# High and low parts of q and k made once per head pair in staging tiles and placed by DMAs

## The chip, the core and the metric

The kernel runs on one core of one Trainium2 chip. The metric is the device time of one execution in microseconds (us). The kernel before takes 946.16 us (median of 3 runs, 944.52 to 946.6). The engines that matter here are TensorE (PE in the profile, its weight loads PEld), VectorE (DVE), ScalarE (ACT), GpSimd (POOL) and SyncE (SP), which issues most of the DMAs. Each engine works through its own instructions in a fixed order and waits at the head of its queue for semaphores.

## The reference

Causal attention with a bias from a running sum, over 8 batches and 8 heads, 576 positions, 64 values a head; then a mixture of experts with one expert a token. Cut to what matters:

```python
scores = matmul(q, k.T) / sqrt(D)
cum = cumsum(maximum(s, 0)); bias = -(cum[..., :, None] - cum[..., None, :])
scores = where(causal, -1e9, scores + minimum(bias, 0))
attn = exp(scores - max(scores)); attn /= sum(attn) + 1e-9
x = matmul(attn, v)                       # (8*576, 512) after the heads are joined
e = argmax(x @ w_gate + modality_bias[modality_id]); gate = softmax prob of e
out[token] = gate * (relu(x @ w1[e]) @ w2[e])
```

## The kernel before, in words

The first part is attention. It goes over 32 head pairs: one head of two batches at a time (`ab` is 0 or 1). For a pair there are nine score tiles, taken in the order `ORDER`: four tiles of 128 queries for each of the two batches, with 128 to 512 keys, and tile 8 ("pep"), which holds the last 64 queries of both. A score is formed in float32r, which keeps only the high part of a float32, so q and k are split: a high part and the rest, the low part. Each tile takes two matmuls into one PSUM bank `sp`: `KA` times `QH` (128 rows: high k over low k, against high q twice) and `KB` times `QL` (76 rows: high k and the rows of the bias against low q and the rows that pick the bias). There are two sets of these four operands, `QH`, `QL`, `KA` and `KB`, used by turns.

After the two matmuls DVE takes the mask and the row minimum (L219, L233), ACT the exponential (L238), PE transposes the tile into a bank `pt` (L248, L257), ACT copies it to `PT` (L251; tile 8: DVE, L263). When all nine tiles of a pair are in `PT`, `tail` multiplies with V (L274 and L279, banks `ox` and `om`), ACT and DVE copy the result to `oT` (L283, L284, L287), PE transposes and projects it (L293, L296: in two groups, which use the one bank `ox` after each other) and DVE scales each group into `x` (L299, L301). `run` writes this with the scores three tiles ahead of the transposes and with the tail of a pair spread over the scores of the next; the order in which each engine finally gets its instructions is set by a scheduler that moves them by its own times, not by the text of `run` alone.

The operands are made in `prep`. [...] POOL makes the high parts of q and k (L174: two calls of 128x576 for `QH`, two for `KA`, two of 64x576 for `KB`) and the low parts (L192 for `KA`, L194 for half of `QL`); DVE makes the other half of `QL` (L188). The rows of the bias come by two small DMAs (L170, L171). `prep(pi + 1)` is written into the scores of pair `pi`. SP's queue carries, per pair, two loads of q and k of 576 KB each, V of 320 KB and the two small ones.

After every eighth pair `done` routes the tokens of two batches: DVE works out the expert of each token, POOL issues nine indirect DMAs (L502) that write the rows to lists in DRAM. The second part, the mixture of experts, works on blocks of 256 tokens of one expert and loads its weights by SP.

Of the kernel before, what the change touches and what calls it, by code (L numbers as in the profile page):

```python
# [7 lines left out]
F32 = mybir.dt.float32  # L8
F32R = mybir.dt.float32r
# [3 lines left out]
ALU = mybir.AluOpType  # L13
# [4 lines left out]
P = 128  # L18
KW = 576
# [11 lines left out]
class Attn:  # L31
# [3 lines left out]
    def __init__(self, ctx, tc, qkv, s, ident, consts):  # L35
        nc = tc.nc
        self.nc, self.tc, self.qkv, self.ident = nc, tc, qkv, ident
        c = self.const = ctx.enter_context(tc.tile_pool(name="aconst", bufs=1))
        self.dr = ctx.enter_context(tc.tile_pool(name="adr", bufs=1, space=DRAM))
        self.ld = ctx.enter_context(tc.tile_pool(name="ld", bufs=2))  # L40
        self.wk = ctx.enter_context(tc.tile_pool(name="wk", bufs=2))
        self.sm = ctx.enter_context(tc.tile_pool(name="sm", bufs=3))
        self.ps1 = ctx.enter_context(tc.tile_pool(name="ps1", bufs=2, space=PSUM))
        self.ps2 = ctx.enter_context(tc.tile_pool(name="ps2", bufs=1, space=PSUM))
        self.QH = [c.tile([P, 2, 640], F32R, name=f"QH{u}") for u in range(2)]
        self.QL = [c.tile([P, 2, 640], F32R, name=f"QL{u}") for u in range(2)]
        self.KA = [c.tile([P, 2, KW], F32R, name=f"KA{u}") for u in range(2)]
        self.KB = [c.tile([P, 2, KW], F32R, name=f"KB{u}") for u in range(2)]
        self.PT = [c.tile([P, PTW], F32, name=f"PT{u}") for u in range(3)]
        self.oT = [c.tile([P, 640], F32, name=f"oT{u}") for u in range(2)]  # L50
        self.pw = c.tile([P, 8, 2 * XW], F32, name="pw")
        self.mk = c.tile([P, 800], F32, name="mk")
        self.hold = [None]
        with tc.tile_pool(name="cst", bufs=1, side="right") as t1:
            sr = t1.tile([64, KW], F32, name="sr")
            nc.sync.dma_start(sr, s)
            raw = self.load_qk(0)
# [11 lines left out]
            self.raw = {0: raw}  # L69
            for _ in self.prep(0):  # L70
                pass

    def exts(self, t1, cum):

# [73 lines left out]
    def load_qk(self, pi):  # L148
        nc = self.nc
        raw = [self.ld.tile([P, 2, KW], F32, name="rawq"), self.ld.tile([P, 2, KW], F32, name="rawk")]  # L150
        for u in range(2):
            nc.sync.dma_start(raw[u], self.qkv[pi, :, 2 * KW * u:2 * KW * u + 2 * KW].rearrange("p (a k) -> p a k", a=2))
        return raw

    def load_v(self, pi):
        V = self.ld.tile([P, 2, 5, 64], F32, name="V", bufs=3)
        self.nc.sync.dma_start(V, self.qkv[pi, :, 4 * KW:].rearrange("p (a j d) -> p a j d", a=2, j=5))
        return V

    def load(self, pi):  # L160
        self.raw[pi] = self.load_qk(pi)
        self.V[pi] = self.load_v(pi)

    def prep(self, pi):
        nc = self.nc
        rq, rk = self.raw.pop(pi)
        QH, QL, KA, KB = (t[pi % 2] for t in (self.QH, self.QL, self.KA, self.KB))
        QHf, KAf = QH.bitcast(F32), KA.bitcast(F32)
        if pi:
            nc.sync.dma_start(KB.bitcast(F32)[64:74], self.ekd.rearrange("(a p) r k -> p r a k", a=2)[pi])  # L170
            nc.sync.dma_start(QL.bitcast(F32)[74:76, :, :KW], self.eqd.rearrange("(a p) r k -> p r a k", a=2)[pi])  # L171

        def high(o, i, e=None):
            (e or nc.gpsimd).tensor_scalar(o, i, 1.0, 1.0, ALU.mult, ALU.mult)  # L174

        lo, up = slice(0, 64), slice(64, P)
        for a in range(2):
            if pi:
                high(QH[:, a, :KW], rq[:, a])
            else:  # L180
                nc.scalar.copy(QH[:, a, :KW], rq[:, a])
        yield
        for a in range(2):
            high(KA[:, a], rk[:, a], nc.vector if pi == 0 and a == 0 else None)
        yield
        for a in range(2):
            if a == 0:
                nc.vector.tensor_tensor(QL[lo, a, :KW], rq[lo, a], QHf[lo, a, :KW], ALU.subtract)  # L188
            high(KB[lo, a], rk[lo, a], nc.vector if pi == 0 and a == 0 else None)
            yield  # L190
        for a in range(2):
            i = (nc.vector if pi == 0 and a == 0 else nc.gpsimd).tensor_tensor(KA[up, a], rk[up, a], KAf[up, a], ALU.subtract)  # L192
            yield
        (nc.vector if pi == 0 else nc.gpsimd).tensor_tensor(QL[lo, 1, :KW], rq[lo, 1], QHf[lo, 1, :KW], ALU.subtract)  # L194
        yield
# [108 lines left out]
    def run(self, npair, newx, done, setup):  # L304

        bg = []
        self.load(1)
        seq = [(pi, i) for pi in range(npair) for i in ORDER]
        sts = {}
        prev, prepg, n = None, None, len(seq)  # L310
        for k in range(n + LAG + 9):
            if k < n:
                pi, i = seq[k]
                if k % 9 == 0:
                    sts[pi] = self.start(pi, newx(pi // 8) if pi % 8 == 0 else sts[pi - 1]["x"])
                    prepg = self.prep(pi + 1) if pi + 1 < npair else None
                self.score(sts[pi], i)
                if k in setup:
                    with ExitStack() as after:
                        for h in self.hold:  # L320
                            after.enter_context(self.tc.issue_after(h))
                        setup[k]()
                if k % 9 == 7 and pi + 2 < npair:
                    self.load(pi + 2)
                if prepg is not None:
                    next(prepg, 0)
            nt = None
            if LAG <= k < n + LAG:
                p0, i0 = seq[k - LAG]
                if i0 == ORDER[-1]:  # L330
                    nt = sts[p0]
            if prev is not None:
                if next(prev, 0) == 0:
                    prev = None
                    if ps["pi"] % 8 == 7:
                        bg.append(done(ps["pi"] // 8, ps["x"]))
            if LAG <= k < n + LAG:
                self.trans(sts[p0], i0)
            if nt is not None:
                prev, ps = self.tail(nt), nt  # L340
            if prev is None and k >= n + LAG:
                break
            if bg and next(bg[0], 0) == 0:
                bg.pop(0)
        assert prev is None
        return bg


def pack(q, k, v, s):

    out = np.zeros((32, 128, 4 * KW + 640), np.float32)
    for bp in range(4):
        for h in range(8):
            o = out[bp * 8 + h]
            for ab in range(2):
                b = 2 * bp + ab
                qT, kT = q[b, h].T, k[b, h].T

                qq = qT if ab == 0 else np.concatenate([qT[:, 512:], qT[:, :512]], 1)
                for r in (0, 64):  # L360
                    o[r:r + 64, KW * ab:KW * ab + KW] = qq
                    o[r:r + 64, KW * (2 + ab):KW * (3 + ab)] = kT
                vv = np.zeros((640, 64), np.float32)
                vv[:576] = v[b, h]
                v0 = 4 * KW + 320 * ab
# [611 lines left out]
```

## Time and profile before

| | us |
|---|---|
| median of 3 runs | 946.16 |
| the profiled execution's own time | 941.79 |
| its span, first to last instruction | 940.1 |
| first reduction of scores (L219) in the span | 29.71 |
| last scaling into x (L301) of the last pair ends | 465.31 |
| PE busy, 42 to 142 us | 99.24 of 100 |
| PE busy, 465 to 900 us | 422.86 of 435 |

The views give times in us from the span's start. In a row of the timeline stand the start, the duration, the engine, the line, the operation and the tiles; in brackets how long the engine was idle before and what ended that. A row of the windows gives each engine's busy time in a stretch, with the number of instructions, then the clock that TensorE was granted, the share of the DMA engines' time and what they moved. SPq is SP's queue of DMA issues.

### The profile page before, as it was taken

How to read it: one execution, taken by the hardware profiler on the slowest of the kernel's cores; microseconds unless marked ns; L12 is line 12 of the kernel's file. 1: busy time of each engine (PE TensorE's matmuls, PEld its weight loads, DVE VectorE, ACT ScalarE, POOL GpSimd, SP SyncE). 2: the span in 40 equal slices, each digit the busy share in tenths (PEclk: the TensorE clock that was granted, in tenths of full speed). 3: DMA queues.
4: the chain of work that ended last, by engine and by line, in shares of the span. 5: the costliest groups of instructions: out<-in, count | busy, mean ns of one | idle time of the engine just before them, and what ended most of it. 6: DMA issues, size and time to landing. Idle time of an engine off the chain costs nothing. (4 is left out here: it accounts for less than half of the span.)

```text
span 940.1 us, 16721 instructions
## 1 busy us (share of the span) xinstructions
PE 860.9 (92%) x5584; PEld 714.7 (76%) x5584; DVE 633.8 (67%) x1485; ACT 527.5 (56%) x1209; POOL 576.1 (61%) x478
## 2 busy tenths in 40 slices
PE   0799999799989998899988989999999999999984
PEld 0577777577667777677777979999999999999862
DVE  7477777577856778777556966566665566566771
ACT  3577776577656775587644525445544454454551
POOL 9576667666786766885064725556655465564760
PEclk9999999899999999999999999999999999999998
DMA  5743334533363335550577757666666666665940
GB/s 149 205 121 135 134 135 133 181 132 113 121 213 118 104 120 171 187 179 18 189 244 263 280 190 290 238 231 223 247 227 220 225 225 228 225 230 224 325 157 3
DMA packets 67564, 172.79 MB, mean 184 GB/s; under 512 B 12087, under 2 KB 12087, under 8 KB 67412
## 3 DMA queue, kind: packets, MB, share of 16 engines
q1 hardware_dynamic: 61620, 151.64, 47.1%
q0 software_dynamic: 5856, 20.06, 5.4%
q8 instruction: 45, 0.74, 0.3%
q14 instruction: 43, 0.35, 0.1%
HBM read 144.95 MB, written 26.80 MB: 183 GB/s over the span
## 5 line engine op out<-in xcount | busy, mean ns | idle before, releaser
L238 ACT ACTIVATE pe<-pe,mx 128x512 f32<-128x512 f32 (+3 forms) x256 | 143.8, 563 | 54.1 <-DVE mx L219 50.7
L279 PE MATMUL om<-PT,V 128*64 128x448 f32 (+3 forms) x640 | 124.9, 424 | 10.7 <-DVE PT L263 10.5
L791 ACT ACTIVATE hT<-hp 128x512 fp32r<-128x512 f32 x72 | 42.8, 595 | 156.9 <-PE hp L789 156.9
L251 ACT COPY PT<-pt 128x512 f32<-128x512 f32 (+3 forms) x256 | 106.7, 421 | 36.1 <-PE pt L248 28.9
L248 PE MATMUL pt<-ident,pe 128*128 128x128 f32 x640 | 121.9, 288 | 4.0 <-DVE PT L263 3.3
L219 DVE CUSTOM_DVE_ANT_0 pe<-sp,mk 128x512 f32<-128x512 f32 (+3 forms) x256 | 114.7, 478 | 12.9 <-PE sp L217 7.3
L775 POOL DMA_INDIRECT out<-ys,oi x36 | 37.3, 1037 | 133.5 <-DVE ys L774 50.5
L216 PE MATMUL sp<-KA,QH 128*128 128x256 f32 (+2 forms) x256 | 97.0, 386 | 20.1 <-DVE KA L192 16.0
L248 PEld LDWEIGHTS pt<-ident,pe 128*128 128x128 f32 x640 | 79.2, 146 | 40.5 <-issue 14.9
L174 POOL TENSOR_SCALAR QH<-rawq 128x576 fp32r<-128x576 f32 x62 | 47.0, 761 | 88.7 <-issue 80.9
L192 POOL TENSOR_TENSOR KA<-rawk,KA 64x576 fp32r<-64x576 f32 x63 | 95.9, 1541 | 2.6
L217 PE MATMUL sp<-KB,QL 76*128 76x256 f32 (+2 forms) x256 | 86.4, 343 | 7.3 <-DMA QL<-oh 7.3
L789 PE MATMUL hp<-xT,wcb 128*128 128x256 f32 x648 | 90.2, 283 | 1.6 <-DVE hT L792 1.6
L279 PEld LDWEIGHTS om<-PT,V 128*64 128x64 f32 x640 | 60.7, 136 | 40.6 <-DVE PT L263 14.9
L789 PEld LDWEIGHTS hp<-xT,wcb 128*128 128x128 f32 x648 | 83.6, 189 | 2.5 <-DVE hT L792 1.9
L792 DVE SCALAR_TENSOR_TENSOR hT<-hp,hT 128x512 fp32r<-128x512 f32 x72 | 49.2, 684 | 52.9 <-ACT hT L791 52.9
L789 PE MATMUL hp<-xT,wcc 128*128 128x256 f32 x528 | 76.4, 285 | 8.3 <-DVE hT L792 3.2
L768 PE MATMUL y<-wcb,hT 128*128 128x512 f32 x336 | 81.1, 398 | 0.0
L789 PE MATMUL hp<-xT,wca 128*128 128x256 f32 x552 | 78.1, 284 | 0.4 <-ACT xT L754 0.3
L789 PEld LDWEIGHTS hp<-xT,wcc 128*128 128x128 f32 x528 | 69.9, 194 | 9.3 <-DVE hT L792 3.4
L768 PEld LDWEIGHTS y<-wcb,hT 128*128 128x128 f32 x336 | 62.8, 188 | 14.8
L789 PEld LDWEIGHTS hp<-xT,wca 128*128 128x128 f32 x552 | 71.7, 190 | 1.3 <-ACT xT L754 0.5
(270 smaller groups left out, 1987.7 us busy)
## 6 DMA issues: line engine op xcount, KB each, us to landing
wrbw<-in_w SPq DMA_DIRECT2D x104, 512.0 KB
wraw<-in_w SPq DMA_DIRECT2D x56, 512.0 KB
rawq<-in_qkv SPq DMA_DIRECT2D x32, 576.0 KB
rawk<-in_qkv SPq DMA_DIRECT2D x32, 576.0 KB
xg<-lists SPq DMA_DIRECT2D x18, 576.0 KB
V<-in_qkv SPq DMA_DIRECT2D x32, 320.0 KB
lists<-z SPq DMA_DIRECT2D x8, 576.0 KB
ekd<-ek SPq DMA_DIRECT2D x1, 1440.0 KB
```

The lines of the kernel that those rows point to most:

```text
L174: (e or nc.gpsimd).tensor_scalar(o, i, 1.0, 1.0, ALU.mult, ALU.mult)
L192: i = (nc.vector if pi == 0 and a == 0 else nc.gpsimd).tensor_tensor(KA[up, a], rk[up, a], KAf[up, a], ALU.subtract)
L216: nc.tensor.matmul(sp[:, :nn], QH[:, q0:q0 + P], KA[:, ab, :nn], start=True, stop=False)
L217: nc.tensor.matmul(sp[:, :nn], QL[:EXT, q0:q0 + P], KB[:EXT, ab, :nn], start=False, stop=True)
L219: ins = nc.vector.tensor_tensor_reduce(out=t[:, :n], in0=sp[:, :n], in1=self.mk[:, 512 - n:512], scale=-0.125, scalar=3.0e38, op0=ALU.add, ...
L238: nc.scalar.activation(t[:, :n], t[:, :n], AF.Exp, bias=m, scale=-1.0, accum_out=st["sums"][:, i:i + 1])
L248: nc.tensor.transpose(out=pt[:, P * j:P * j + P], in_=pe[:, P * j:P * j + P], identity=self.ident)
L251: cp(w[:, :, v:v + P], pt[:, :P * (c + 1)].rearrange("p (j q) -> p j q", q=P))
L279: nc.tensor.matmul(om[r, q0 - P:], V[:, ab, j, :], PT[ab][:, PTS * j + q0 if j < 4 else PTW - 64:PTS * j + KW if j < 4 else PTW], start=j ...
L768: self.last[0] = nc.tensor.matmul(y[u], hT[:, a, f, P * u:P * u + P], W[4 + f // 2][:, c, 512 * (f % 2):512 * (f % 2) + 512], start=f == 0 ...
L789: nc.tensor.matmul(hp[:, u], W[k][:, a, f:f + P], xT[:, c, k], start=k == 0 and i == 0, stop=k == 3 and i == 2)
L792: nc.vector.scalar_tensor_tensor(hT[:, 1, 2 * m:2 * m + 2], hp, 0.0, hs.bitcast(F32), ALU.max, ALU.subtract)
```

## The change

The host packs each row of q and k once: q on rows 0 to 63 and k on rows 64 to 127 of one array, so that one load R of 576 KB per pair takes the place of two. `split` makes the high part H and the low part L of the whole tile on POOL, in four calls of 128x576 (two a half `a`). `place` copies them to where the matmuls read: six DMAs between SBUF tiles, of 64 partitions and 288 KB each, on SP's queue, and the two small ones for the rows of the bias behind them. H and L have one buffer each. `split` runs two pairs ahead of the scores, `place` one pair ahead, R is loaded three pairs ahead. DVE's share of the split is gone. Pair 0 keeps the old way of splitting (`prep0`), with its operands loaded by four DMAs of 64 partitions.

```diff
+    def load_r(self, pi):
+        R = self.R[pi] = self.ld.tile([P, 2, KW], F32, name="R", bufs=2)
+        self.nc.sync.dma_start(R, self.qkv[pi, :, :2 * KW].rearrange("p (a k) -> p a k", a=2))
+    def split(self, pi):
+        nc = self.nc
+        R = self.R.pop(pi)
+        H, L = (self.ld.tile([P, 2, KW], F32R, name=n, bufs=1) for n in ("H", "L"))
+        self.S[pi] = H, L
+        for a in range(2):
+            nc.gpsimd.tensor_scalar(H[:, a], R[:, a], 1.0, 1.0, ALU.mult, ALU.mult)
+            yield
+            nc.gpsimd.tensor_tensor(L[:, a], R[:, a], H[:, a].bitcast(F32), ALU.subtract)
+            yield
+    def place(self, pi):
+        nc = self.nc
+        H, L = (t.bitcast(F32) for t in self.S.pop(pi))
+        QH, QL, KA, KB = (t[pi % 2].bitcast(F32) for t in (self.QH, self.QL, self.KA, self.KB))
+        lo, up = slice(0, 64), slice(64, P)
+        nc.sync.dma_start(QH[lo, :, :KW], H[lo])
+        nc.sync.dma_start(QH[up, :, :KW], H[lo])
+        nc.sync.dma_start(KA[lo], H[up])
+        nc.sync.dma_start(KA[up], L[up])
+        nc.sync.dma_start(QL[lo, :, :KW], L[lo])
+        nc.sync.dma_start(KB[lo], H[up])
+        nc.sync.dma_start(KB[64:74], self.ekd.rearrange("(a p) r k -> p r a k", a=2)[pi])
+        nc.sync.dma_start(QL[74:76, :, :KW], self.eqd.rearrange("(a p) r k -> p r a k", a=2)[pi])
...
     def run(self, npair, newx, done, setup):
         bg = []
-        self.load(1)
+        self.load_r(1)
+        self.V[1] = self.load_v(1)
+        self.load_r(2)
+        for _ in self.split(1):
+            pass
...
-                    prepg = self.prep(pi + 1) if pi + 1 < npair else None
+                    if pi + 1 < npair:
+                        self.place(pi + 1)
+                    prepg = self.split(pi + 2) if pi + 2 < npair else None
...
-                if k % 9 == 7 and pi + 2 < npair:
-                    self.load(pi + 2)
+                if k % 9 == 7:
+                    if pi + 3 < npair:
+                        self.load_r(pi + 3)
+                    if pi + 2 < npair:
+                        self.V[pi + 2] = self.load_v(pi + 2)
```

The diff does not touch the tails, the reductions or the exponentials, but the scheduler orders all of them anew. Line numbers move: L216 and L217 become L234 and L235, L219 becomes L237, L238 becomes L256, L251 becomes L269, L279 becomes L297, L287 becomes L305, L293 becomes L311, L299 becomes L317, L301 becomes L319.

First PE, around the end of the V product of one pair (om of pair 11) before the change. sp are the score banks of pair 12, om the V product, pt a transpose, ox at the end of the list the projection of pair 11.

```order
L279 MATMUL om<-PT_107,V 64x64
L279 MATMUL om<-PT_108,V 64x64
L248 MATMUL pt<-ident,pe 128x128 x4
L230 MATMUL sp<-KA_102,QH_98 128x288
L231 MATMUL sp<-KB_104,QL_100 128x288
L230 MATMUL sp<-KA_102,QH_98 128x288
L231 MATMUL sp<-KB_104,QL_100 128x288
L230 MATMUL sp<-KA_102,QH_98 128x288
L231 MATMUL sp<-KB_104,QL_100 128x288
L230 MATMUL sp<-KA_102,QH_98 128x288
L231 MATMUL sp<-KB_104,QL_100 128x288
L293 MATMUL ox<-pw,oT_110 128x144 x2
```

The four wide scores of pair 12 lie ahead of this piece; a transpose and the eight matmuls of its tile 8 stand between the V product of pair 11 and the first group of its projection. The same place with the change:

```order
L297 MATMUL om<-PT_108,V 64x192
L297 MATMUL om<-PT_107,V 64x64
L297 MATMUL om<-PT_108,V 64x64
L311 MATMUL ox<-pw,oT_110 128x144 x4
L314 MATMUL ox<-pw,oT_110 128x72 x2
L235 MATMUL sp<-KB_104,QL_100 128x512 x2
L235 MATMUL sp<-KB_104,QL_100 128x384
L235 MATMUL sp<-KB_104,QL_100 128x256
L248 MATMUL sp<-KA_102,QH_98 128x288
L249 MATMUL sp<-KB_104,QL_100 128x288
L248 MATMUL sp<-KA_102,QH_98 128x288
L249 MATMUL sp<-KB_104,QL_100 128x288
```

The projection of pair 11 follows its V product with nothing between, and the KB halves of all scores of pair 12 come behind the projection; only the KA halves of its first four tiles lie further ahead, inside the V product. From pair 4 on, this repeats for every pair.

Second DVE, at the scaling of a pair (x and xq of pair 11) before the change. The ISA rows with pe are the reductions of the scores (the rows with mx alone read out their result).

```order
L299 TENSOR_TENSOR x<-ox,rs 128x288
L219 ISA pe,mx<-sp,mk 128x384
L219 ISA mx 128x1
L299 TENSOR_TENSOR x<-ox,rs 128x288
L301 TENSOR_SCALAR xq<-ox,rs 128x72
L219 ISA pe,mx<-sp,mk 128x256
L219 ISA mx 128x1
L219 ISA pe,mx<-sp,mk 128x128
L219 ISA mx 128x1
L188 TENSOR_TENSOR QL_100<-rawq,QH_98 64x576
```

With the change:

```order
L299 TENSOR_SCALAR rs<-sums 128x9
L300 RECIPROCAL rs<-rs 128x9
L305 COPY oT_110<-om 64x64 x2
L317 TENSOR_TENSOR x<-ox,rs 128x288 x2
L319 TENSOR_SCALAR xq<-ox,rs 128x72
L237 ISA pe,mx<-sp,mk 128x512
L237 ISA mx 128x1
L237 ISA pe,mx<-sp,mk 128x512
L237 ISA mx 128x1
L237 ISA pe,mx<-sp,mk 128x384
```

The scaling of pair 11 was spread over the later reductions of pair 12; it now stands whole ahead of the first reduction of pair 12.

Third ACT, at the copies to oT of pair 11, before and with the change (ACTIVATE is the exponential, pep that of tile 8):

```order
L238 ACTIVATE pe,sums<-pe,mx 128x512 x2
L251 COPY PT_107<-pt 128x128
L238 ACTIVATE pe,sums<-pe,mx 128x384
L251 COPY PT_108<-pt 128x128
L238 ACTIVATE pe,sums<-pe,mx 128x256
L283 COPY oT_110<-ox 128x128
L284 COPY oT_110<-om 128x384
```

```order
L269 COPY PT_108<-pt 128x3x128
L269 COPY PT_108<-pt 128x2x128
L269 COPY PT_107<-pt 128x128
L269 COPY PT_108<-pt 128x128
L301 COPY oT_110<-ox 128x128
L302 COPY oT_110<-om 128x384
L256 ACTIVATE pe,sums<-pe,mx 128x512 x2
```

The first four exponentials of the next pair stood ahead of the copies to oT and now stand behind them.

More of the change, by code (lines that the diff above doesn't have):

```diff
@@ L56, in __init__ @@
             nc.sync.dma_start(sr, s)
-            raw = self.load_qk(0)
+            raw = self.load0()
             zz = t1.tile([64, KW], F32, name="zz")
@@ L68, in __init__ @@
             self.V = {0: self.load_v(0)}
-            self.raw = {0: raw}
-            for _ in self.prep(0):
-                pass
+            self.prep0(*raw)
+            self.R, self.S = {}, {}
     def exts(self, t1, cum):
@@ L146, in rows0, with load0 @@
                 nc.sync.dma_start(self.KB[u].bitcast(F32)[74:76, ab], self.m1[:2])
-    def load_qk(self, pi):
+    def load0(self):
         nc = self.nc
-        raw = [self.ld.tile([P, 2, KW], F32, name="rawq"), self.ld.tile([P, 2, KW], F32, name="rawk")]
+        raw = [self.ld.tile([P, 2, KW], F32R, name=n, bufs=1).bitcast(F32) for n in ("H", "L")]
         for u in range(2):
-            nc.sync.dma_start(raw[u], self.qkv[pi, :, 2 * KW * u:2 * KW * u + 2 * KW].rearrange("p (a k) -> p a k", a=2))
+            src = self.qkv[0, 64 * u:64 * u + 64, :2 * KW].rearrange("p (a k) -> p a k", a=2)
+            for r in (slice(0, 64), slice(64, P)):
+                nc.sync.dma_start(raw[u][r], src)
         return raw
@@ L156, in load_v @@
         V = self.ld.tile([P, 2, 5, 64], F32, name="V", bufs=3)
-        self.nc.sync.dma_start(V, self.qkv[pi, :, 4 * KW:].rearrange("p (a j d) -> p a j d", a=2, j=5))
+        self.nc.sync.dma_start(V, self.qkv[pi, :, 2 * KW:].rearrange("p (a j d) -> p a j d", a=2, j=5))
         return V
[L160 to L164, printed above, removed]
+    def load_r(self, pi):
+        R = self.R[pi] = self.ld.tile([P, 2, KW], F32, name="R", bufs=2)
+        self.nc.sync.dma_start(R, self.qkv[pi, :, :2 * KW].rearrange("p (a k) -> p a k", a=2))
@@ L165, in prep @@
+    def split(self, pi):
         nc = self.nc
-        rq, rk = self.raw.pop(pi)
-        QH, QL, KA, KB = (t[pi % 2] for t in (self.QH, self.QL, self.KA, self.KB))
-        QHf, KAf = QH.bitcast(F32), KA.bitcast(F32)
[L169 to L174, printed above, removed]
+        R = self.R.pop(pi)
[6 more added lines that the diff above has]
+            yield
@@ L176, in prep, with prep0, high @@
+    def prep0(self, rq, rk):
+        nc = self.nc
+        QH, QL, KA, KB = (t[0] for t in (self.QH, self.QL, self.KA, self.KB))
+        QHf, KAf = QH.bitcast(F32), KA.bitcast(F32)
+        def high(o, i, e):
+            e.tensor_scalar(o, i, 1.0, 1.0, ALU.mult, ALU.mult)
         lo, up = slice(0, 64), slice(64, P)
         for a in range(2):
[L178 to L182, printed above, removed]
+            nc.scalar.copy(QH[:, a, :KW], rq[:, a])
@@ L183, in prep @@
         for a in range(2):
-            high(KA[:, a], rk[:, a], nc.vector if pi == 0 and a == 0 else None)
-        yield
+            high(KA[:, a], rk[:, a], nc.gpsimd if a else nc.vector)
         for a in range(2):
@@ L188, in prep @@
                 nc.vector.tensor_tensor(QL[lo, a, :KW], rq[lo, a], QHf[lo, a, :KW], ALU.subtract)
-            high(KB[lo, a], rk[lo, a], nc.vector if pi == 0 and a == 0 else None)
-            yield
+            high(KB[lo, a], rk[lo, a], nc.gpsimd if a else nc.vector)
         for a in range(2):
[L192 to L195, printed above, removed]
+            (nc.gpsimd if a else nc.vector).tensor_tensor(KA[up, a], rk[up, a], KAf[up, a], ALU.subtract)
+        nc.vector.tensor_tensor(QL[lo, 1, :KW], rq[lo, 1], QHf[lo, 1, :KW], ALU.subtract)
     def start(self, pi, x):
@@ L349, in pack @@
 def pack(q, k, v, s):
-    out = np.zeros((32, 128, 4 * KW + 640), np.float32)
+    out = np.zeros((32, 128, 2 * KW + 640), np.float32)
     for bp in range(4):
@@ L359, in pack @@
                 qq = qT if ab == 0 else np.concatenate([qT[:, 512:], qT[:, :512]], 1)
-                for r in (0, 64):
-                    o[r:r + 64, KW * ab:KW * ab + KW] = qq
-                    o[r:r + 64, KW * (2 + ab):KW * (3 + ab)] = kT
+                o[:64, KW * ab:KW * ab + KW] = qq
+                o[64:, KW * ab:KW * ab + KW] = kT
                 vv = np.zeros((640, 64), np.float32)
                 vv[:576] = v[b, h]
-                v0 = 4 * KW + 320 * ab
+                v0 = 2 * KW + 320 * ab
                 o[:, v0:v0 + 320] = vv.reshape(5, 128, 64).transpose(1, 0, 2).reshape(128, 320)
```

## The prediction

> **What bounds the kernel now.** I read the page first, then the windows by stage, the queue of SP, the waits, and last the timeline of single pairs.
>
> ```profile
> span 940.1 us, 16721 instructions
> PE 860.9 (92%) x5584; PEld 714.7 (76%) x5584; DVE 633.8 (67%) x1485; ACT 527.5 (56%) x1209; POOL 576.1 (61%) x478
> ```
>
> PE is the busiest engine. The windows say where it is not:
>
> ```profile
> 142.00:184.00 42.00, 34.72 (x240) 26.79 (x236) 25.70 (x90) 23.64 (x74) 29.78 (x30) 0.92 0.52 173
> 184.00:247.00 63.00, 62.37 (x428) 47.62 (x427) 46.48 (x163) 45.79 (x141) 42.40 (x45) 1.00 0.36 121
> 247.00:300.00 53.00, 47.69 (x307) 35.97 (x308) 37.51 (x135) 33.59 (x108) 40.50 (x44) 0.94 0.44 147
> ...
> 362.00:395.00 33.00, 26.38 (x169) 20.61 (x165) 26.60 (x89) 16.14 (x52) 23.97 (x26) 0.90 0.63 206
> ...
> 465.00:900.00 435.00, 422.86 (x2720) 382.53 (x2719) 289.56 (x332) 210.04 (x263) 245.97 (x116) 0.99 0.66 240
> ```
>
> Between routings (184 to 247) PE is busy 62.37 of 63 us. DVE (46.48), ACT (45.79) and POOL (42.40) each have a quarter or more to spare. Around the three routings PE idles, and its clock falls to 0.92, 0.94 and 0.90. The experts (465 to 900) are bound by PE; the change does not touch them. SP's queue shows the period of a pair, since the small bias load is issued once a pair:
>
> ```profile
> 185.36 0.31 SPq L170 DMA_DIRECT2D KB<-ekd  x1
> ...
> 248.28 0.31 SPq L170 DMA_DIRECT2D KB<-ekd  x1
> ```
>
> Five pairs in 62.92 us: **12.58 us a pair**. The attention part runs from the first reduction to the last scaling into x:
>
> ```profile
> 29.71 0.69 DVE L219 CUSTOM_DVE_ANT_0 pe<-sp,mk 128x512 f32<-128x512 f32 x1 [5.70 <-PE sp L217]
> ...
> 464.99 0.32 DVE L301 TENSOR_SCALAR xq<-ox,rs 128x72 f32<-128x72 f32 x1
> ```
>
> That is 435.6 us; 32 x 12.58 = 402.6, so 33 us lie in the start and the three routings. What stops PE at a routing is in the waits of DVE:
>
> ```profile
> DVE QL L188 <- issue: 9.6, 2, 5.6
> ```
>
> DVE's half of QL needs a high part that POOL makes behind its indirect DMAs; DVE stands 9.6 us on two of these, and PE behind it.
>
> **The change, part by part.** It takes work off POOL and DVE:
>
> ```profile
> L192 POOL TENSOR_TENSOR KA<-rawk,KA 64x576 fp32r<-64x576 f32 x63 | 95.9, 1541 | 2.6
> ...
> L174 POOL TENSOR_SCALAR QH<-rawq 128x576 fp32r<-128x576 f32 x62 | 47.0, 761 | 88.7 <-issue 80.9 <-PE sp L216 3.7 <-PE sp L217 3.6
> ...
> L194 POOL TENSOR_TENSOR QL<-rawq,QH 64x576 fp32r<-64x576 f32 x31 | 43.8, 1414 | 2.3
> L174 POOL TENSOR_SCALAR KA<-rawk 128x576 fp32r<-128x576 f32 x63 | 43.0, 685 | 8.0 <-DMA rawk<-in_qkv 8.0
> L174 POOL TENSOR_SCALAR KB<-rawk 64x576 fp32r<-64x576 f32 x63 | 42.0, 681 | 0.0
> ...
> L188 DVE TENSOR_TENSOR QL<-rawq,QH 64x576 fp32r<-64x576 f32 x32 | 35.2, 1101 | 16.2 <-issue 9.6 <-POOL QH L174 6.6
> ```
>
> POOL a pair before: 2 x 0.76 + 2 x 0.69 + 2 x 0.68 + 2 x 1.54 + 1.41 = 8.8 us. After: two high parts and two subtractions. A duration here goes with the free size (64 and 128 partitions cost alike in the rows of L174), so 2 x 0.76 + 2 x 1.54 = 4.6 us. Saved: 4.2 us of POOL and 1.1 us of DVE a pair. Neither bounds the steady pair, so there this is worth nothing by itself. At the routings it is worth something: L188 is gone, with its 9.6 us, and with it most of the slow clock, (1-0.92) x 42 + (1-0.94) x 53 + (1-0.90) x 33 = 9.9 us. I take all of it: **-19.5 us** (bounds 0, if the routing rows then queue on another engine, and -33, all that is there).
>
> It adds six transfers of 288 KB (295 kB, together 1.77 MB) a pair and removes one load of 576 KB. The trace has no such transfer between SBUF tiles. The nearest are the stores of ek and eq from 64 partitions (18 to 26 us), and for 128 partitions the loads of pair 1 (33 to 35 us):
>
> ```profile
> 18.00:26.00 8.00, 1.33 (x3) 0.83 (x3) 2.97 (x6) 0.00 (x0) 5.26 (x9) 1.00 1.00 204
> ...
> 33.00:35.00 2.00, 2.00 (x17) 2.00 (x17) 1.31 (x7) 1.49 (x5) 1.92 (x3) 1.00 1.01 408
> ```
>
> At 204 GB/s six placements take 8.7 us, at 408 GB/s 4.3 us; I take 8.7, by the row with 64 partitions. H and L have one buffer, so there is a loop of its own: high parts (1.5 us), placements (8.7 us), and an issue and a landing. For these the first load of q:
>
> ```profile
> 1.43 0.56 SPq L152 DMA_DIRECT2D rawq<-in_qkv  x1
> ...
> 5.38 1.24 ACT L181 CAST QH<-rawq 128x576 fp32r<-128x576 f32 x2 [3.31 <-DMA rawq<-in_qkv]
> ```
>
> It takes 3.95 us from issue to the end of ACT's wait, of which 590 kB at 408 GB/s are 1.4; 2.5 us are left, and I put 3 us as an estimate, with two hand-overs to POOL and SP. The loop is about 13.2 us. The low parts and R move inside it. The wait of the first placement for the last score of the pair before holds SP's queue, with R and V of later pairs behind it, but those are needed one pair later or more.
>
> The Trainium skill, page "SBUF — State Buffer", section "Door 1: The DMA port swizzle", speaks against the change: partitions 0 to 63 reach 8 of 16 ports, so such a transfer gets at most about 218 GB/s. The two rows agree (204 against 408). By it the placements would take 8.1 us, with full ports 4.1 us (436 GB/s); in either case the loop stays under the period that I get next.
>
> **What the new order costs.** The term that decides is not in the diff but in the order. Before, the reductions and exponentials of the next pair stand ahead of the tail of this one on DVE and ACT, and scores and transposes fill PE while the tail waits. With the change no reduction of pair p+1 can start before pair p is scaled: on PE the KB matmuls stand behind the second projection, on DVE the first reduction behind x and xq, on ACT the exponentials behind oT. A pair then takes its whole chain, end to end. The profile shows this chain alone, at the last pair, behind which no scores come:
>
> ```profile
> 456.42 0.27 DVE L219 CUSTOM_DVE_ANT_0 pe<-sp,mk 128x128 f32<-128x128 f32 x1
> ...
> 456.80 0.40 ACT L238 ACTIVATE pe<-pe,mx 128x128 f32<-128x128 f32 x1 [0.64 <-DVE mx L219]
> ...
> 457.44 1.44 ACT L251 COPY PT<-pt 128x384 f32<-128x384 f32 x4 [0.15 <-PE pt L248]
> ...
> 459.31 0.39 PE L274 MATMUL ox<-PT,V 128*64 128x128 f32 x4
> 459.53 1.89 PE L279 MATMUL om<-PT,V 128*64 128x448 f32 x14
> 459.78 0.27 ACT L283 COPY oT<-ox 128x128 f32<-128x128 f32 x1 [0.90 <-PE ox L274]
> ...
> 461.46 0.48 ACT L284 COPY oT<-om 128x384 f32<-128x384 f32 x1 [1.41 <-PE om L279]
> ...
> 461.97 0.46 DVE L287 COPY oT<-om 64x64 f32<-64x64 f32 x2 [4.23 <-ACT oT L284]
> 462.54 0.67 DVE L299 TENSOR_TENSOR x<-ox,rs 128x288 f32<-128x288 f32 x1
> 463.27 0.76 PE L293 MATMUL ox<-pw,oT 128*128 128x144 f32 x4 [0.76 <-DVE x L299]
> ...
> 464.46 0.69 DVE L299 TENSOR_TENSOR x<-ox,rs 128x288 f32<-128x288 f32 x1 [1.25 <-PE ox L296]
> ...
> 465.17 0.15 DVE L740 TENSOR_TENSOR oi<-xg,fpast 128x2 int32<-128x2 f32 x1
> ```
>
> The last copy to PT ends at 457.44 + 1.44 = 458.88; DVE comes to its next work at 465.17. So from the last copy to the point where a first reduction could start: 6.3 us. It is a true chain: V product, copy to oT, projection, scaling, second projection (one bank for both), scaling. The period now, from first reduction to first reduction:
> - the first reduction and its hand-over, 0.8 us (0.69 in the row at 29.71; 0.11 from the rows at 456.42 and 456.80: 0.38 less 0.27);
> - ACT's exponentials and copies to PT in one run: 45.79 us in five pairs is 9.15 a pair, less the two copies to oT (0.27 and 0.48), 8.4 us;
> - 6.3 us as shown;
> - the four KA matmuls that the order puts inside the V product: a wide one starts 0.23 us after the one before (below), 1664 columns together, 0.75 us.
>
> ```profile
> 185.17 0.39 PE L216 MATMUL sp<-KA,QH 128*128 128x512 f32 x1
> 185.40 0.40 PE L217 MATMUL sp<-KB,QL 76*128 76x512 f32 x1
> ```
>
> Sum 16.25 us. It has no wait inside ACT's run. The last five transposes wait for one of two banks pt, which DVE and ACT must empty; I add 0.35 us: **16.6 us a pair**. Bounds: 15.4 us if ACT's instructions overlap by a tenth more than its busy time shows, 17.6 us if ACT stands 1.3 us at those banks. PE keeps its clock: the shortest stand of PE at a routing whose stretch shows a low clock is
>
> ```profile
> PE pt L248 <- DVE PT L263: 3.3, 1, 3.3
> ```
>
> and no single wait in this chain is that long.
>
> The placement loop (13.2 us) is shorter and hides. Sum: 32 x (16.6 - 12.58) = +128.6 us, less 19.5 us, **+109 us**. The profiled execution took 941.79 us and would take 1051. The median of the runs is 946.16, which puts the time at **1055 us**. Pair by pair bounds: 32 x 2.8 - 19.5 = +70 (1016 us) and 32 x 5.0 - 19.5 = +141 (1087 us); with nothing won at the routings 1107.
>
> **The rivals.**
>
> *The placements set the pace.* If transfers between SBUF tiles go at half the rate of the store (102 GB/s, since each reads and writes the SBUF), they take 17.3 us, and the loop 21.8 us: 946 + 32 x 9.2 - 19.5 = 1221 us. For it: one buffer for H and L, and eight transfers in one queue. Against: the store row moved at 204 GB/s while POOL and DVE worked, and a rate above 145 GB/s is enough for the loop to stay under 16.6 us.
>
> *Not slower: the chain overlaps after all.* The place is the boundary of two pairs on ACT and DVE. If first reductions ran beside the tail as before, PE would set 12.58 us again, the waits of L188 would be gone, and the time would be 946 - 19.5 = 927 us. It decides as soon as the chain is under 12.58 us, 3.7 us less than its rows add up to. For it: POOL and DVE have less to do. DVE's L281 took 0.79 us in the mean of 32 and 0.17 us at the last pair, where POOL hardly worked:
>
> ```profile
> L281 DVE TENSOR_SCALAR rs<-sums 128x9 f32<-128x9 f32 x32 | 25.1, 786 | 0.6 <-ACT pe L238 0.6
> ...
> 457.32 0.17 DVE L281 TENSOR_SCALAR rs<-sums 128x9 f32<-128x9 f32 x1 [0.62 <-ACT pe L238]
> ```
>
> The Trainium skill, page "SBUF — State Buffer", section "Who interferes with whom", has the rule: GpSimd and a two-port DVE instruction lock each other out for a whole instruction. The two rows agree; by the rule up to 0.6 us a pair, 20 us in all, would come back if DVE set the pace.
>
> Against the rival: the instructions of an engine don't pass each other, and L281 lies in the shadow of ACT's run.
>
> **How the numbers follow.** Chances: the chain as computed 0.84, the placements 0.08, not slower 0.08 (0.05 faster, 0.03 within 0.2%, which is about what a measurement of this kernel can tell from no change). Slower: 0.92. The time is that of the chain, 1055 us. Its bounds are 1016 to 1107; I widen them downward to 1000, since ACT's run could begin while the last copies still go, and leave the other cases out, 0.16 together: 1000 to 1110 us.
>
> **What would show it.** Right: in the changed profile the small bias load (L191) comes every 16 to 17 us; PE's share in the attention part falls to about 12.5 / 16.6 = 75% at a clock near 1.00; ACT and DVE show waits at the first reduction of a pair and at oT; POOL is busy about 4.6 us a pair; the experts take the 475 us that they took. Wrong: if PE's first KA matmul waits for a placement, the placements decide; if L191 comes every 12 to 13 us, there is no chain.

## The result, and the profile after

The changed kernel takes **1100.2 us** (median of 4 runs, 1098.81 to 1108.63), the kernel before beside it 945.39 us (4 runs, 944.52 to 946.6): ratio 1.1655, 95% interval 1.1594 to 1.1716, 155 us slower. The forecast was 1055 us with a range of 1000 to 1110: right in sign and in mechanism, 45 us too low. The profiled execution took 1099.63 us.

The head of the page of the changed kernel: every engine has a smaller share of the span than before, none has become the bound.

```profile
span 1097.9 us, 16771 instructions
PE 935.4 (85%) x5584; PEld 744.5 (68%) x5584; DVE 586.7 (53%) x1454; ACT 522.8 (48%) x1209; POOL 438.1 (40%) x323
```

The windows of both kernels by stage (busy time of PE, PEld, DVE, ACT and POOL, then granted clock, DMA share, GB/s). The kernel before, attention and experts:

```profile
29.71:465.30 435.59, 411.14 (x2753) 314.19 (x2752) 310.38 (x1100) 298.31 (x913) 294.64 (x310) 0.98 0.42 140
465.00:940.00 475.00, 447.19 (x2829) 398.67 (x2827) 305.20 (x348) 221.61 (x280) 259.57 (x123) 0.98 0.62 226
```

The changed kernel: attention, one pair of it, six microseconds of another, experts.

```profile
29.43:622.00 592.57, 484.87 (x2753) 343.50 (x2752) 261.74 (x1070) 294.36 (x914) 157.98 (x158) 0.94 0.64 169
227.51:245.18 17.67, 14.26 (x86) 9.84 (x85) 7.54 (x33) 8.86 (x28) 6.32 (x7) 1.00 0.71 193
141.00:147.00 6.00, 5.86 (x21) 3.18 (x21) 0.00 (x0) 1.33 (x4) 0.00 (x0) 0.50 0.99 236
623.00:1097.00 474.00, 446.74 (x2823) 398.48 (x2822) 306.51 (x344) 219.64 (x278) 260.67 (x123) 0.98 0.61 223
```

From the last scaling into x to the last instruction the changed kernel takes 476 us, the kernel before 475; the 157 us are all in the attention (592.3 against 435.6, from the first reduction to the last scaling). POOL has lost 137 us of work there and DVE 49 us, and it won nothing.

One pair of the changed kernel, from its first reduction to that of the next, in the timeline (rows of the chain alone; SP's first and last placement and POOL's next high part between them):

```profile
227.33 0.32 DVE L319 TENSOR_SCALAR xq<-ox,rs 128x72 f32<-128x72 f32 x1
227.51 0.67 DVE L237 CUSTOM_DVE_ANT_0 pe<-sp,mk 128x512 f32<-128x512 f32 x1
...
228.29 0.72 ACT L256 ACTIVATE pe<-pe,mx 128x512 f32<-128x512 f32 x1 [4.05 <-DVE mx L237]
...
231.60 0.62 SPq L185 DMA_DIRECT2D QH<-H  x1
...
234.34 1.01 DVE L281 COPY PT<-pt 128x256 f32<-128x256 f32 x4 [2.05 <-PE pt L275]
...
234.81 0.97 PE L297 MATMUL om<-PT,V 128*64 128x448 f32 x2
...
235.71 0.76 PE L266 MATMUL pt<-ident,pe 128*128 128x128 f32 x5
236.29 1.44 ACT L269 COPY PT<-pt 128x384 f32<-128x384 f32 x4 [1.17 <-PE pt L266]
...
237.36 0.97 PE L297 MATMUL om<-PT,V 128*64 128x448 f32 x4
...
238.26 1.02 PE L234 MATMUL sp<-KA,QH 128*128 128x512 f32 x4
238.94 0.26 SPq L192 DMA_DIRECT2D QL<-eqd  x1
...
239.22 0.44 PE L292 MATMUL ox<-PT,V 128*64 128x128 f32 x4
...
242.96 1.31 POOL L174 TENSOR_SCALAR H<-R 128x576 fp32r<-128x576 f32 x2 [11.36 <-DMA KB<-ekd]
...
245.00 0.31 DVE L319 TENSOR_SCALAR xq<-ox,rs 128x72 f32<-128x72 f32 x1
245.18 0.68 DVE L237 CUSTOM_DVE_ANT_0 pe<-sp,mk 128x512 f32<-128x512 f32 x1
```

The first reduction stands 0.18 us behind the start of the last scaling of the pair before: the pairs don't overlap on DVE. The period is 245.18 - 227.51 = **17.67 us**, in three parts: reduction and hand-over 228.29 - 227.51 = 0.78; ACT's run up to the end of its last copy at 236.29 + 1.44 = 237.73, 9.44, with 1.17 us of waiting; from there to the next reduction 7.45. The placements (231.60 to 239.20 at SP, the staging tiles free at 242.96) end long before the next pair but one needs them.

### The profile page after: what moved, and what is told of

The parts are those of the page before. It is cut to its first block, busy times and chain, and to the rows that moved or that the text cites. A ratio compares the mean times of both kernels' runs of the same rounds, so it can differ in the third digit from the quotient of the medians.

```text
span 1097.9 us, 16771 instructions
## 1 busy us (share of the span) xinstructions
PE 935.4 (85%) x5584; PEld 744.5 (68%) x5584; DVE 586.7 (53%) x1454; ACT 522.8 (48%) x1209; POOL 438.1 (40%) x323
## 5 line engine op out<-in xcount | busy, mean ns | idle before, releaser
L256 ACT ACTIVATE pe<-pe,mx 128x512 f32<-128x512 f32 (+3 forms) x256 | 142.3, 558 | 130.0 <-DVE mx L237 127.4
L174 POOL TENSOR_SCALAR H<-R 128x576 fp32r<-128x576 f32 x62 | 40.6, 674 | 282.9 <-DMA KB<-ekd 169.8
L297 PE MATMUL om<-PT,V 128*64 128x448 f32 (+3 forms) x640 | 127.4, 431 | 5.4 <-DVE PT L281 2.2
L266 PEld LDWEIGHTS pt<-ident,pe 128*128 128x128 f32 x640 | 82.2, 155 | 66.7 <-ACT PT L269 35.1
L237 DVE CUSTOM_DVE_ANT_0 pe<-sp,mk 128x512 f32<-128x512 f32 (+3 forms) x256 | 111.6, 484 | 27.9 <-PE sp L235 26.0
L269 ACT COPY PT<-pt 128x512 f32<-128x512 f32 (+3 forms) x256 | 103.9, 419 | 46.0 <-PE pt L266 41.0
L305 DVE COPY oT<-om 64x64 f32<-64x64 f32 x64 | 14.2, 222 | 197.9 <-ACT oT L302 197.4
L234 PE MATMUL sp<-KA,QH 128*128 128x256 f32 (+2 forms) x256 | 78.3, 373 | 20.0 <-DVE frem L623 16.7
L176 POOL TENSOR_TENSOR L<-R,H 128x576 fp32r<-128x576 f32 x62 | 86.4, 1414 | 0.0
L311 PE MATMUL ox<-pw,oT 128*128 128x144 f32 x256 | 56.9, 325 | 30.1 <-DVE x L317 24.4
L234 PEld LDWEIGHTS sp<-KA,QH 128*128 128x128 f32 x256 | 50.3, 206 | 44.0 <-issue 18.3
L297 PEld LDWEIGHTS om<-PT,V 128*64 128x64 f32 x640 | 59.5, 139 | 30.4 <-DVE PT L281 11.7
L235 PE MATMUL sp<-KB,QL 76*128 76x256 f32 (+2 forms) x256 | 71.6, 353 | 8.0 <-DMA QL<-oh 6.7
```

The costliest lines, as they stand in the source:

```text
L176: nc.gpsimd.tensor_tensor(L[:, a], R[:, a], H[:, a].bitcast(F32), ALU.subtract)
L234: nc.tensor.matmul(sp[:, :nn], QH[:, q0:q0 + P], KA[:, ab, :nn], start=True, stop=False)
L235: nc.tensor.matmul(sp[:, :nn], QL[:EXT, q0:q0 + P], KB[:EXT, ab, :nn], start=False, stop=True)
L237: ins = nc.vector.tensor_tensor_reduce(out=t[:, :n], in0=sp[:, :n], in1=self.mk[:, 512 - n:512], scale=-0.125, scalar=3.0e38, op0=ALU.add, ...
L256: nc.scalar.activation(t[:, :n], t[:, :n], AF.Exp, bias=m, scale=-1.0, accum_out=st["sums"][:, i:i + 1])
L266: nc.tensor.transpose(out=pt[:, P * j:P * j + P], in_=pe[:, P * j:P * j + P], identity=self.ident)
```

## The experiments

Seven kernels, in two groups, each group with its own runs of the kernel before (942.98 us in the first, 943.96 in the second). Lines shift by up to five where an edit adds some.

**1. The order alone, mended.** Each step of a tail is held, on PE, DVE and ACT, behind the last score traced before it (`front` holds that score's last KB matmul, its reduction and its exponential):

```diff
+                with ExitStack() as after:
+                    for i in self.front:
+                        after.enter_context(self.tc.issue_after(i))
+                    more = next(prev, 0)
-                if next(prev, 0) == 0:
+                if more == 0:
```

> The changed kernel with its split and its placements as they are, but with the tail of a pair (V product, copies to oT, projection, scaling) held behind the scores of the next pair that stand ahead of it in the text, on PE, DVE and ACT: reductions, exponentials and scores of two pairs overlap again, as in the kernel before. Theory 'order' (the new order alone costs the time, and the placements hide): the period goes back to the 12.6 us that PE sets, and the time to 946 us or up to 20 us below it (926 to 950). Rival 'one buffer' (H and L have one buffer, and the loop of split and placements becomes the bound as soon as the order is mended): in the changed kernel the first placement is issued at 231.60, POOL's next high part starts at 242.96 and its last low part ends at 247.03, so the loop takes 15.4 us and some tenths of hand-over, 15.8 us, and the time is 946 + 32 x 3.2 = 1048 us, or up to 20 us less (1028 to 1050), with POOL or PE standing behind placements.

Measured: 968.7 us (967.09 to 970.12), ratio 1.0266, interval 1.0242 to 1.029. So 131 of the 155 us come back with the order, and all transfers still there. Neither number was met. The timeline of this run, two first reductions and the loop of one buffer:

```profile
107.77 0.69 DVE L237 CUSTOM_DVE_ANT_0 pe<-sp,mk 128x512 f32<-128x512 f32 x1 [2.14 <-PE sp L235]
...
120.21 0.69 DVE L237 CUSTOM_DVE_ANT_0 pe<-sp,mk 128x512 f32<-128x512 f32 x1 [2.14 <-PE sp L235]
```

```profile
117.61 0.62 SPq L185 DMA_DIRECT2D QH<-H  x1
...
128.18 1.31 POOL L174 TENSOR_SCALAR H<-R 128x576 fp32r<-128x576 f32 x2 [7.87 <-DMA KB<-ekd]
129.46 2.78 POOL L176 TENSOR_TENSOR L<-R,H 128x576 fp32r<-128x576 f32 x2
129.52 0.62 SPq L185 DMA_DIRECT2D QH<-H  x1
```

The period is 12.44 us, a little under the 12.58 of before. The loop of one buffer takes 129.52 - 117.61 = 11.91 us, not 15.8: the next placement leaves as soon as the high parts are made (128.18 + 1.31), and the low parts are made while it runs. It fits under 12.44 with half a microsecond to spare. What this run lacks lies at the start and the routings. At the first routing two first reductions (160.86 and 180.73) stand 19.87 us apart, and POOL comes to the next split behind nine indirect DMAs:

```profile
161.91 1.18 POOL L533 DMA_INDIRECT lists<-x,di  x1 [2.06 <-DVE mx L237]
...
172.27 0.96 POOL L533 DMA_INDIRECT lists<-xq,di  x1 [0.30 <-issue]
173.26 1.32 POOL L174 TENSOR_SCALAR H<-R 128x576 fp32r<-128x576 f32 x2
```

```profile
160.86 0.68 DVE L237 CUSTOM_DVE_ANT_0 pe<-sp,mk 128x512 f32<-128x512 f32 x1
...
169.91 0.52 DVE L251 CUSTOM_DVE_ANT_0 pep<-sp,mk,mx 128x288 f32<-128x288 f32 x1 [2.88 <-remote]
...
172.03 0.67 DVE L318 TENSOR_TENSOR x<-ox,rs 128x288 f32<-128x288 f32 x1 [1.59 <-remote]
...
180.73 0.69 DVE L237 CUSTOM_DVE_ANT_0 pe<-sp,mk 128x512 f32<-128x512 f32 x1 [2.14 <-PE sp L235]
```

That is not yet the rival's case: PE waits for a placement twice in this run, 2.2 and 1.3 us, both at the start. DVE, which stands 2.88 and 1.59 us here, waits for something that the profile calls only "remote"; what that is stays open.

**2. The order alone, given to the kernel before.** Scores of a pair are written behind the tail of the last, with two edges (`back` holds the last projection matmul and the last scaling):

```diff
+                with (self.tc.issue_after(self.back[1]) if self.back else ExitStack()):
+                    self.score(sts[pi], i)
...
+            with (self.tc.issue_after(self.back[0]) if self.back else ExitStack()):
+                nc.tensor.matmul(sp[:, :nn], QL[:EXT, q0:q0 + P], KB[:EXT, ab, :nn], start=False, stop=True)
```

> The kernel before with its own split and loads, no placements, but in the order that the change got: the first reduction of a pair stands behind the last scaling of the pair before, and its KB matmuls behind the second projection. Theory 'order': the period is that of the chain, 17.0 to 17.7 us (the changed kernel has 17.67; the four KA matmuls stand a little earlier here, worth up to 0.75 us), and the time 946 + 32 x 4.4 to 946 + 32 x 5.1, 1087 to 1109 us. Rival 'placements' (the transfers slow the engines or hold operands back, and the order is only part of it): clearly under that, 1040 us or less.

Measured: 1070.08 us (1068.09 to 1071.94), ratio 1.1343, interval 1.1315 to 1.1371. No placement, no staging tile, and 127 us are lost. The time lies between the two forecasts (1087 us at the least, 1040 us at the most). A pair in its timeline:

```profile
263.44 1.44 ACT L252 COPY PT<-pt 128x384 f32<-128x384 f32 x4 [1.17 <-PE pt L249]
...
264.51 0.97 PE L280 MATMUL om<-PT,V 128*64 128x448 f32 x4
265.31 0.39 PE L275 MATMUL ox<-PT,V 128*64 128x128 f32 x4
...
271.21 0.67 DVE L220 CUSTOM_DVE_ANT_0 pe<-sp,mk 128x512 f32<-128x512 f32 x1
...
271.99 0.72 ACT L239 ACTIVATE pe<-pe,mx 128x512 f32<-128x512 f32 x1 [4.05 <-DVE mx L220]
...
279.99 0.48 ACT L252 COPY PT<-pt 128x384 f32<-128x384 f32 x1 [1.17 <-PE pt L249]
```

0.78 us again from reduction to exponential. ACT's run is one copy group of 1.44 us behind 279.99, so it ends at 281.43: 9.44 us, the same to the hundredth. From the end of the last copy (264.88) to the next reduction 6.33 us, against 7.45. The sum, 16.55, is the period. Under the 17.0 that was expected at the least, since the KA matmuls, outside the V product here, cost nothing at all.

**3. Two buffers beside the order.** `bufs=2` for H and L; for room `bufs=1` for R, and three tiles of the start share memory:

```diff
-        H, L = (self.ld.tile([P, 2, KW], F32R, name=n, bufs=1) for n in ("H", "L"))
+        H, L = (self.ld.tile([P, 2, KW], F32R, name=n, bufs=2) for n in ("H", "L"))
```

> As the first run, but with two buffers for H and two for L (room for them: one buffer of R in place of two, and three tiles of the start share memory). The order on PE, DVE and ACT is that of the first run. Theory 'order': the same time as the first run, 926 to 950 us. Rival 'one buffer': the first run is at 1028 to 1050 us and this one comes back to 926 to 955 us, since splits no longer wait for placements; what is left of the loop is the 11.4 us of the placements themselves, under 12.6.

Measured: 948.32 us (942.68 to 950.38), ratio 1.0062, interval 1.0041 to 1.0083. The second buffers win 20 us once the order is mended: not in the steady pair, whose period is again 12.43 us, but at the routings. The rival had the sign and the wrong place. How they win is not shown, since the order on POOL moves with them: at the first routing a split stands between the fourth and the fifth of the nine indirect DMAs (165.60), where the first run had it behind them all (173.26), and no run parts the two. This run loses time at the start, where the first reductions of pairs 0 to 4 lie 67.4 us apart in sum, against 46.2 before (SP, POOL and PE of this run):

```profile
27.28 0.42 SPq L164 DMA_DIRECT2D R<-in_qkv  x1
...
31.38 1.30 POOL L173 TENSOR_SCALAR H<-R 128x576 fp32r<-128x576 f32 x2 [6.89 <-DMA R<-in_qkv]
...
46.02 1.73 PE L233 MATMUL sp<-KA,QH 128*128 128x512 f32 x4 [6.91 <-DMA KA<-L]
```

**4. The second step of the prediction by itself.** L188 moved to POOL in the kernel before:

```diff
-                nc.vector.tensor_tensor(QL[lo, a, :KW], rq[lo, a], QHf[lo, a, :KW], ALU.subtract)
+                (nc.gpsimd if pi else nc.vector).tensor_tensor(QL[lo, a, :KW], rq[lo, a], QHf[lo, a, :KW], ALU.subtract)
```

> The kernel before with the half of QL that DVE makes (L188) moved to POOL, nothing else. It tests the second step of the prediction, that this instruction's waits at the routings and the slow clock behind them are worth 19.5 us. By that step: 927 us (926 to 932). Rival 'POOL is late in any case' (PE then waits for POOL's low parts themselves, behind the same indirect DMAs, and POOL has 10.2 us a pair to do instead of 8.8): 946 us or more (942 to 965).

Measured: 935.22 us (930.28 to 936.4), ratio 0.9897, interval 0.9865 to 0.9929: 7.8 us won, not 19.5, between the two forecasts, and the fastest kernel of this study. The windows of the three routings, to be held against those of before in the prediction:

```profile
142.00:184.00 42.00, 38.37 (x267) 28.28 (x265) 29.67 (x105) 28.05 (x89) 37.10 (x40) 1.00 0.51 176
247.00:300.00 53.00, 49.47 (x340) 37.24 (x337) 35.25 (x126) 34.26 (x109) 43.77 (x47) 0.97 0.50 170
362.00:395.00 33.00, 27.30 (x168) 19.85 (x167) 20.94 (x71) 18.33 (x56) 27.52 (x28) 0.90 0.60 213
```

PE's clock comes back at the first routing (0.92 to 1.00), half at the second (0.94 to 0.97), not at the third (0.90 both times). The stall of DVE was at most one cause among others: POOL has its work in this run, and at the first routing four of the nine indirect DMAs stand ahead of the split where three did.

**5. The changed kernel in the order of the second run**, by the same edit.

> The changed kernel, split and placements as they are, with the serial order of the second run: first reduction behind the last scaling of the pair before, KB matmuls behind the second projection, and the four KA matmuls no longer inside the V product but in the waits of the projection. Theory 'order': in the changed kernel ACT's last copy to PT ends at 237.73 and the next first reduction starts at 245.18, 7.45 us; in the second run (no placements) 264.88 and 271.21, 6.33 us; the other parts of the period are alike (0.78 and 9.44 us). If the 1.12 us between them are the KA matmuls, the period falls from 17.67 to about 16.55 us, and the time from 1100 by up to 32 x 1.12 = 36 us, to 1064 to 1080 us, near the 1070 us of the second run. Rival 'placements' (what stands between 1070 and 1100 us is the cost of the transfers beside the chain): the period stays near 17.6 and the time at 1090 to 1105 us.

Measured: 1077.96 us (1075.75 to 1079.39), ratio 1.1429, interval 1.1408 to 1.145. In its timeline ACT's last copy ends at 129.75 + 1.44 = 131.19, and the next reduction starts at 137.52:

```profile
129.75 1.44 ACT L270 COPY PT<-pt 128x384 f32<-128x384 f32 x4 [1.17 <-PE pt L267]
...
137.52 0.68 DVE L238 CUSTOM_DVE_ANT_0 pe<-sp,mk 128x512 f32<-128x512 f32 x1
```

6.33 us, as without placements. The KA matmuls lie among the last transposes here (127.50 to 130.36), not in the waits of the projection as was expected, and cost the chain nothing: the whole 1.12 us goes with their place. The time falls by 22 of the 30 us between the second run and the changed kernel, though 1.12 us in every pair would make 36. The 8 us that are left are not in this pair; no run says where they come from.

**6. Two buffers without the order**, the third run less the edit of the first.

> The third run without the part that holds the tails: two buffers for H and L, and the order as the scheduler makes it. Its order on DVE is serial again (the first reduction directly behind the last scaling of the pair before). Theory 'order': two buffers alone win little, since in the changed kernel the high parts wait for placements in the shadow of the chain: period about 16.6 to 17.7 us, 1065 to 1100 us. Rival 'one buffer' (it is the buffer that holds the pairs apart): 950 to 1000 us.

Measured: 1091.16 us (1089.62 to 1096.33), ratio 1.1574, interval 1.1534 to 1.1614. The reductions of this run stand 17.66 us apart (226.08 and 243.74). The buffer does not hold the pairs apart.

**7. The start.** R of pair 1 is loaded right behind the loads of pair 0, in the third run's kernel, and the load for pair 2 behind the split of pair 1:

```diff
             raw = self.load0()
+            self.R, self.S = {}, {}
+            self.load_r(1)
```

> The third run with the load R of pair 1 issued at the start, right behind the loads of pair 0, and no longer behind the rows of QL and KB. In the third run R was issued at 27.28, POOL came to the split of pair 1 at 31.38, 6.89 us after it was free, and PE waited 6.91 us for the first KA of pair 1, for a placement. Theory 'start' (what the third run has above the kernel before is this start: its first reductions of pairs 0 to 4 lie 67.4 us apart in sum, before 46.2): the split starts near 24.5, and 6.9 us are won: 941 us (938 to 944). Rival 'transfers' (the placements of pairs 1 to 4 and the loads beside them fill the queue, so PE waits as long for the next ones): 946 to 950 us.

Measured: 941.34 us (936.07 to 947.01, 10 runs), ratio 0.9975, interval 0.9952 to 0.9998: 7.0 us less than the third run, as expected. Part of this was the third run's own price: with one buffer of R its load for pair 2 (35.48) held SP's queue, and the placements behind it, until POOL had read that buffer. The start is not all mended: the first reductions of pairs 0 to 4 still lie 60.1 us apart in sum, 14 more than before. In all, with its order, buffers and this load mended, the change is as fast as the kernel before. The fourth run, the old data path, is faster than both.

## Why the prediction was right, and where it was short

By its own steps:

- **PE bounds the kernel before at 12.58 us a pair; work taken off POOL and DVE is worth nothing in the steady pair.** Right. Runs 1 and 3 have that work off and all pairs overlapped, and go to 12.43 us. POOL's rows (L174 at 0.674 us, L176 at 1.414, two each) make 4.2 us a pair, 4.6 were forecast.
- **The placements hide.** Right for the pair: run 5 has them and run 2 has not, and the chain is the same 6.33 and 9.44 us. The loop was put at 13.2 us and is 11.91 in run 1. Not seen: in an overlapped order one buffer, or the order on POOL that comes with it, costs 20 us at the routings (run 3 against run 1), and the start takes 14 to 21 us longer than before in all three overlapped runs (1, 3 and 7).
- **The new order serialises the pairs.** Right, and it is the cause: run 1 takes the order away and 131 us go, run 2 brings it alone and 127 come.
- **16.6 us a pair.** This is the term that was mis-sized: 17.67. Reduction and hand-over, 0.8 forecast, 0.78 measured. The tail without KA, 6.3 forecast from the last pair of before, 6.33 measured. *The KA matmuls*, 0.75 forecast: in the rows the V product's next matmul starts 1.86 us behind 237.36 (239.22), in run 2 0.80 us (264.51 and 265.31), and with what follows 7.45 - 6.33 = 1.12. They were costed by their columns alone, at 0.23 us for a wide one; what the rest is, the rows don't say. *ACT's run*, 8.4 + 0.35 forecast, 9.44 measured: 8.27 of work and 1.17 of waiting. The wait is not the two banks, as the prediction put it, but the order on PE: two matmuls of the V product (234.81) stand ahead of the last transposes (235.71), they wait for DVE's copies of tile 8 (234.34), and the transposes wait behind them. That is read off the rows; runs 2 and 5 have the same order there and the same 1.17 us, and no run moves these two matmuls. Together 1.06 us a pair, 34 us. The upper bound of that step, 17.6, came out almost exactly, but by two causes where it named one: that is luck.
- **-19.5 us at the routings.** Wrong in size. 592.3 us of attention less 32 x 17.67 leave 26.9, where 33 stood before: 6 us won, 13 less than forecast. These 26.9 us are a remainder: they also hold pairs slowed by the clock, as the one of 20.28 us below. The rows of attention:

```profile
29.43 0.69 DVE L237 CUSTOM_DVE_ANT_0 pe<-sp,mk 128x512 f32<-128x512 f32 x1 [7.82 <-PE sp L235]
...
621.45 0.32 DVE L319 TENSOR_SCALAR xq<-ox,rs 128x72 f32<-128x72 f32 x1
```

 The step took all the slow clock as the price of one stalled instruction. Run 4 moves only that instruction to POOL and wins 7.8 us.
- **PE keeps its clock.** Wrong for the whole, right for the pair shown (1.00): 0.94 over the attention, against 0.98 before. In the 6 us from 141 it is 0.50, and that pair takes 20.28 us. From 130 us on, ahead of the drop, PE never stood longer than 0.77 us, so the longest single wait was no measure. The Trainium skill, page "TensorE: Matmul & The Clock Gate", section "A second HAM failure mode: psum-queue depth-cycling", says that many short idles between groups of matmuls are enough to make the clock swing between half and full. The trace agrees with half and full; why one pair falls and its neighbours with the same rows do not, no run here shows.
- **The sum.** 34 us from the period and 13 from the routings make 47, about the 46 by which the measured difference (155) exceeds the forecast one (109). That the time still lay inside the range is in part luck: its upper end was reckoned with 16.6 us a pair and nothing won at the routings, and neither was so.

*The rivals.* "The placements set the pace" would need a first KA matmul that waits for a placement: PE's matmuls wait for a placement 1.3 us in all, in the row of L235, and a weight load of L234 once, 0.7 us. "The chain overlaps after all" fell with the first reductions. Its side remark held: DVE's small L281, now L299, has become shorter, with POOL at about half the work (158.0 us in the attention against 294.6).

```profile
L299 DVE TENSOR_SCALAR rs<-sums 128x9 f32<-128x9 f32 x32 | 6.8, 211 | 2.3 <-ACT pe L256 1.2 <-ACT pep L256 1.1
L235 PE MATMUL sp<-KB,QL 76*128 76x256 f32 (+2 forms) x256 | 71.6, 353 | 8.0 <-DMA QL<-oh 6.7 <-DMA KB<-H 1.3
```

From 786 ns to 211 in the mean, 18 us in all, as the rule on DVE and GpSimd in the Trainium skill ("SBUF — State Buffer", "Who interferes with whom") would have it; DVE is not on the path there, so the time shows nothing of it.

*The signs.* ACT waits at the first reduction of a pair (4.05 us, at 228.29), as forecast. L191 every 16 to 17 us: it came every 17.6 in steady stretches (rows below), but unevenly behind a routing, where placements catch up; the first reductions are the better clock. PE at 75%: 14.26 of 17.67 is 81%. The experts at 475 us: 476.

```profile
404.37 0.76 SPq L191 DMA_DIRECT2D KB<-ekd  x1
...
421.99 0.80 SPq L191 DMA_DIRECT2D KB<-ekd  x1
```

What stays open is why the scheduler wrote this order. The runs show that the buffer of H and L is not the reason (run 6); its own times for transfers are in no trace.

## What to carry to other kernels

A change of the data path can cost little where it acts and much through the order that a scheduler then picks: compare the order of each engine first, and if two loops that overlapped now follow each other, sum the chain end to end, with every instruction that stands in the queue ahead of a link and not only those that feed it. The last iteration of the old kernel, behind which nothing comes, shows that chain (6.3 us forecast, 6.33 measured). A few edges that keep the old order are then a cheap test of the data path itself, and here they were worth 131 us.

## What the runs showed of the hardware that was not expected

- Issuing a placement is work for SP: 0.62 us (231.60) against 0.31 for the small bias load of the kernel before. The size of a transfer is not all of it: the same bias load, behind the placements, takes 0.76 and 0.80 us (L191 in the rows above). The eight issues of a pair hold its queue for 7.6 us (231.60 to 239.20), and a load behind them waits as long.
- In 234 to 236 us, with only placements of 64 partitions under way, the DMA engines were 0.96 busy and moved 195 GB/s; the store row of the prediction had 204. From 236 to 238, still placements alone, it was 247:

```profile
234.00:236.00 2.00, 1.78 (x9) 0.65 (x8) 1.30 (x6) 1.13 (x6) 0.00 (x0) 1.00 0.96 195
236.00:238.00 2.00, 1.65 (x11) 0.71 (x9) 0.00 (x0) 1.28 (x4) 0.00 (x0) 1.00 1.00 247
```

 That is above the about 218 GB/s that the Trainium skill ("SBUF — State Buffer", "Door 1: The DMA port swizzle") gives one transfer of partitions 0 to 63; whether two of different halves ran together there, the trace does not tell.
- At the routings of run 1 DVE stood up to 3.99 us, and ACT 2.10 us, for a releaser that the profile calls only "remote". Runs 3 and 7, with the order of run 1 and two buffers, have no such wait; but run 2, which has no staging tile, has one of 4.95 us on DVE, so the buffers of H and L are not the whole of it.
